# One core's GELU feed-forward: the last 64 rows of w1 loaded to both partition halves, tiles paired across halves, and w1's first piece cut by rows

## The chip, the cores and the metric

The kernel runs on one core of a Trainium2 chip. The metric is the device time of one execution in microseconds (us); of several runs the median counts. Below, PE is the matrix engine, PEld its weight loads, DVE the vector engine, ACT the scalar engine, POOL GpSimd, and SP the engine that issues most transfers. A transfer "lands" when its semaphore says that all of it has been written.

## The reference

```python
B, S, D, F = 1, 2048, 448, 1792          # all tensors bf16
h = jnp.einsum("bsd,df->bsf", x, w1) + b1
h = jax.nn.gelu(h, approximate=True)
out = jnp.einsum("bsf,fd->bsd", h, w2) + b2
```

D is 448, which is three blocks of 128 rows and 64 rows more. F is 14 blocks of 128.

## The kernel before, in words

**The work.** The 2048 tokens are taken in four chunks of 512 (SC). For a chunk, layer 1 makes 14 tiles of h (128 of F by 512 tokens), which go in seven pairs; a pair shares a unit of PSUM, and there are four units. ACT applies the GELU with the bias b1 and writes g. Layer 2 multiplies g by w2 for the chunk's four blocks of 128 tokens, DVE adds b2, and SP stores.

**Two halves.** Every matmul uses 64 rows: partitions 0 to 63 or 64 to 127. Two matmuls on different halves run side by side. So the two tiles of a pair always work on opposite halves: in pass "a" of `Layer1.step` tile lo works on one half, in pass "b" on the other. Rows 0 to 383 of w1 are three full blocks (k = 0, 1, 2), and both halves are needed by both tiles. The last 64 rows (k = 3) are a single half block, multiplied in pass "b" alone: one tile of the pair has them on the lower half of the partitions, the other on the upper half. The matching rows of x stand on both halves.

**The last 64 rows of w1 before.** `load_w1r` (line 135) brings them to partitions 64 to 127 alone, in two pieces (64 KB and 160 KB). The copies of line 399 on DVE then move the odd tiles of each piece to partitions 0 to 63 (events w1rU), since a pair is tiles 2j and 2j+1 and its odd tile works on the lower half in pass "b".

**Order.** Each engine has a list of operations that is written out by hand and carried out in order; an operation waits for the named events (`Program.emit`, line 45). A transfer has a semaphore of its own per event, and a wait is for the full count. The lists that matter here:

- SP, from line 153: x of chunk 0 (`xn`), then a barrier until ACT's table load is over, `load_w1r(0)`, `load_w1(2)` (tiles 4 to 7), `load_w1r(1)`, `load_w1(3)` (tiles 8 to 13), the two halves of w2, b2, and twelve transposing loads for x of chunks 1 to 3.
- ACT issues `load_w1(0)` (tiles 0, 1) and `load_w1(1)` (tiles 2, 3) at its start. POOL issues the load of b1.
- PE, from line 389: eight warming matmuls on ones (`warm`), the transposes of x (`turn_first`), pair 0's pass "a" on the first 256 tokens (HC), the rest of the transposes (`turn_rest`), pair 1's pass "a" on the same tokens, both passes on the next 256 tokens, then pass "b" of pairs 0 and 1, and from pair 2 on `L[j].a()` followed by `L[j - 1].b()`.
- DVE and ACT empty the transposes from PSUM into xT (`drain_blocks`, line 357, and line 384). DVE then does the first copy of line 399, the turning of b1 (`turn_b1`, line 179), and the second copy of line 399.

All matmuls of the two layers are recorded at line 217, the weight loads too; the transposes at line 344; the warming at line 192; the GELU at line 269.

Of the kernel before, what the change touches and what calls it, by code (L numbers as in the profile page):

```python
# [7 lines left out]
BF16 = mybir.dt.bfloat16  # L8
# [65 lines left out]
def bass_standalone__dense_activation_gelu__prompt_kernel(  # L74
# [8 lines left out]
    B, S, D = x.shape  # L83
    F = w1.shape[1]
    P = 128
    H = P // 2
    SC = 512
    HC = SC // 2
    assert B == 1 and S % SC == 0 and F == 14 * P and D == 3 * P + H
    x2, out2 = x[0], out[0]  # L90
    NSC, NST, STC, NFT = S // SC, S // P, SC // P, F // P
    NPAIR = NFT // 2
    KT = 3
    D3 = KT * P
# [3 lines left out]
    with ExitStack() as es:  # L98
        sb = lambda name, shape, dt: es.enter_context(nc.sbuf_tensor(name, shape, dt))
# [2 lines left out]
        ident = sb("ident", [P, P], BF16)  # L102
        xT = sb("xT", [P, KT + 1, S], BF16)
        w1_sb = sb("w1_sb", [P, KT, F], BF16)
        w1r = sb("w1r", [P, F], BF16)
        w2_sb = sb("w2_sb", [P, NFT, D], BF16)
        junk = sb("junk", [P, 1], BF16)
        b1n = sb("b1n", [32, P], BF16)
# [8 lines left out]
        pr = Program(nc, es)  # L117
# [2 lines left out]
        ones_m = one.broadcast_to([P, SC])  # L120


        W1CUTS = (0, 2, 4, 8, 14)

        def w1_of(ft):
            return max(i for i, c in enumerate(W1CUTS) if c <= ft)

        def load_w1(i, engine="sync"):
            c0, c1 = W1CUTS[i] * P, W1CUTS[i + 1] * P
            pr.dma(engine, lambda e: e.dma_start(  # L130
                w1_sb[:, :, c0:c1], w1[0:D3, c0:c1].rearrange("(k p) f -> p k f", p=P)), ("w1", i))

        RCUTS = (0, 4, 14)

        def load_w1r(i, engine="sync"):
            cs = slice(RCUTS[i] * P, RCUTS[i + 1] * P)
            pr.dma(engine, lambda e: e.dma_start(w1r[H:P, cs], w1[D3:D, cs]), ("w1r", i))

        def load_w2(a, b):
            pr.dma("sync", lambda e: e.dma_start(  # L140
                w2_sb[:, a:b, :], w2[a * P:b * P, :].rearrange("(f p) d -> p f d", p=P)), ("w2", a))
# [11 lines left out]
        pr.dma("sync", lambda e: e.dma_start(xn[:, :, :], x0v), "x")  # L153
        pr.barrier("sync", ["table"])
        load_w1r(0)
        load_w1(2)
        load_w1r(1)
        load_w1(3)
        load_w2(0, 7)
        load_w2(7, 14)  # L160
        pr.dma("sync", lambda e: e.dma_start(b2_bc[:, :], b2.partition_broadcast(P)), "b2")
        for c in range(1, NSC):
            for slot in range(KT + 1):
# [9 lines left out]
        pr.dma("gpsimd", lambda e: e.dma_start(b1n[0:NFT, :], b1.rearrange("(c p) -> c p", p=P)), "b1n",  # L173
               after=["b1z"])
        pr.op("scalar", lambda e: e.activation(junk[:, :], one, ACT.Gelu_apprx_tanh), event="table")  # L175
        load_w1(0, "scalar")
        load_w1(1, "scalar")

        def turn_b1():
            for q in range(4):  # L180
                pr.op("vector", lambda e, q=q: e.transpose(  # L181
                    b1t[32 * q:32 * q + 32, :], b1n[:, 32 * q:32 * q + 32]), after=["b1n"], event=("b1t", q))
            pr.op("vector", lambda e: e.tensor_copy(b1_f[:, :], b1t[:, 0:NFT]),
                  after=[("b1t", q) for q in range(4)], event="b1")
# [21 lines left out]
        def free(u):  # L206
            return [busy[(u, i)] for i in (0, 1, 2) if (u, i) in busy]

        def mm(u, lo, half, cols, lhsT, rhs, start, stop, after, event=None, skip=False):

            after = list(after)
            before = side.get((u, lo))
            if start:
                before = None
            if before is not None and before[0] != half:
                after.append(before[1])
            o = pr.op("tensor", lambda e: e.matmul(  # L217
                unit[u][:, lo, cols], lhsT=lhsT, rhs=rhs, start=start, stop=stop, skip_group_check=skip),
                after=after, event=event)
            side[(u, lo)] = (half, o)  # L220

        class Layer1:
# [6 lines left out]
            def step(self, part, k, t0=0, t1=SC):  # L229
                c, j, u = self.c, self.j, self.u  # L230
                s0 = c * SC
                for lo in (0, 1):
                    ft = 2 * j + lo
                    half = lo if part == "a" else 1 - lo
                    rows = slice(half * H, (half + 1) * H)
                    if k < KT:
                        lhsT = w1_sb[rows, k, ft * P:(ft + 1) * P]
                        after = [("w1", w1_of(ft))]
                    else:
                        lhsT = w1r[rows, ft * P:(ft + 1) * P]  # L240
                        after = [("w1r" if half else "w1rU", int(ft >= RCUTS[1]))]
                    if c == 0:
                        for h in range(t0 // HC, t1 // HC):
                            after += ([("xT0", h, k)] if k < KT else
                                      [("xR0", half, 0), ("xR0", half, 1)])
                    else:
                        after += [("xT", c), ("xTd", c)]
                    if self.fresh:
                        after += free(u)
                    fin = part == "b" and k == KT and t1 == SC  # L250
                    mm(u, lo, half, slice(t0, t1), lhsT, xT[rows, k, s0 + t0:s0 + t1], self.fresh, fin, after,
                       ("h", c, ft) if fin else None, self.skip)
                self.fresh = False
# [11 lines left out]
            def act(self):  # L265
                c, u = self.c, self.u
                for lo in (0, 1):
                    ft = 2 * self.j + lo
                    pr.op("scalar", lambda e, lo=lo, ft=ft: e.activation(  # L269
                        g[:, ft, c * SC:(c + 1) * SC], unit[u][:, lo, :], ACT.Gelu_apprx_tanh,  # L270
                        bias=b1_f[:, ft:ft + 1], scale=1.0), after=[("h", c, ft), "b1"], event=("g", c, ft))
                    busy[(u, lo)] = ("g", c, ft)
# [99 lines left out]
        def turn_rest():  # L372


            turn_block(1, 2, 2, 0, [("xT0", 0, 2)])
            for q in range(STC // 2):
                turn(lambda half, q=q: spot(2, 1)[:, half, q, :], lambda rows, q=q: xr[rows, q, :], ("xr", q), ["xr_in"])
            drain_blocks("vector", 1, (2,), 2, ("xr", 1))
            for src, engine in enumerate(("vector", "scalar")):
                i = spot(2, 1, HALVES[src])  # L380
                for dst in (src, 1 - src):
                    o = xT[HALVES[dst], KT, 0:SC].rearrange("p (q two b s) -> p b q two s", q=2, two=2, b=2)[:, :, :, src, :]
                    pr.op(engine, lambda e, o=o, i=i, engine=engine:
                          e.copy(o, i) if engine == "scalar" else e.tensor_copy(o, i),  # L384
                          after=[("xr", 1), ("xT0", 1, 2)], event=("xR0", dst, src))
            busy[(2, 1)] = ("xR0", 1, 0)
            busy[(2, 2)] = ("xR0", 0, 1)
# [2 lines left out]
        warm(1, HC)  # L390
        turn_first()
        L = [Layer1(0, j) for j in range(NPAIR)]
        L[0].a(0, HC)
        turn_rest()

        for i in (0, 1):
            odd = lambda rows, i=i: w1r[rows, RCUTS[i] * P:RCUTS[i + 1] * P].rearrange(
                "p (j two q) -> p j two q", two=2, q=P)[:, :, 1, :]
            pr.op("vector", lambda e, odd=odd: e.tensor_copy(odd(slice(0, H)), odd(slice(H, P))),
                  after=[("w1r", i)], event=("w1rU", i))  # L400
            if i == 0:
                turn_b1()
        L[1].a(0, HC)
        L[0].a(HC, SC)
        L[1].a(HC, SC)
        L[0].b()
# [7 lines left out]
        for c in range(NSC):  # L414
            if c:
                items = [Layer1(c, j) for j in range(NPAIR)]
                items[0].a()
                for j in range(1, NPAIR):
                    items[j].a()
                    items[j - 1].b()  # L420
                items[-1].b()
            else:

                pr.op("vector", lambda e: e.tensor_copy(b2_z[H:H + 1, :], b2_bc[H:H + 1, :]),  # L424
                      after=["b2", "b2z0"], event="b2z")
            if c + 1 < NSC:
                dup_x((c + 1) * SC, (c + 2) * SC, [("xT", c + 1)], ("xTd", c + 1))
            head, tail, every = range(0, 10), range(10, NFT), range(NFT)
            p = Layer2(c, (0, 1))
            if c + 1 < NSC:  # L430
                q = Layer2(c, (2, 3))
                for part in (head, tail):
                    p.part("a", part)
                    q.part("a", part)
                p.part("b", every)
                q.part("b", every)
            else:
                q, r = Layer2(c, (2,)), Layer2(c, (3,), True)
                p.part("a", every)
                q.part("a", every)  # L440
                p.part("b", every)
                r.bias()
                r.part("a", every)
                q.part("b", every)
                r.part("b", every)
# [30 lines left out]
```

## Time and profile before

| what | value |
|---|---|
| median of 11 runs | 93.89 us (93.82 to 94.46) |
| the profiled execution's own time | 93.82 us |
| its span, first to last instruction | 92.5 us |
| time around the span | 93.82 - 92.5 = 1.3 us |
| PE busy | 89.2 us, 945 matmuls |
| ACT busy / DVE busy | 38.4 us / 13.5 us |
| moved by DMA | 7.32 MB; HBM read 3.79 MB, written 1.84 MB |
| granted PE clock | 1.000 |

How to read it: the profile lists each engine's instructions with start and duration in us from the start of the span, and for idle time before an instruction it names what released it. A start in the table of line 217 is one matmul of a pair; its partner on the other half starts a few ns later, and durations of neighbours overlap, so progress on PE is read from the distance between starts, not from single durations. For transfers there are the issuing instruction (queue SPq, ACTq or POOLq), the time from issue to landing, and, behind the queue view, a record of every packet (one contiguous run moved by one DMA engine: start, duration, bytes) and of every landing (sixteen for a load, the last one releases the waiter).

### The profile page before, as it was taken

The page shows a single profiled execution, that of the slowest core. Times are in us where ns is not written, and L with a number is a line of the kernel's source. Part 1 is how long each engine was busy: PE and PEld are TensorE (multiplying, and loading weights), DVE is VectorE, ACT ScalarE, POOL GpSimd, SP SyncE. Part 2 cuts the span into 40 slices and gives each one's busy share as a digit, 9 for nine tenths or more (in the row PEclk, how much of TensorE's full clock was granted, in tenths as well). Part 3 has the DMA queues.
Part 4 walks back from the last instruction along what each step waited for, and adds up shares of the span by engine and source line. Part 5 has one row for each costly group of instructions (what it writes and reads, how often), then busy time and mean ns, then how long its engine had stood idle before and what let it go on. Part 6 is the DMA issues. An engine that isn't in the chain of part 4 may idle for free.

```text
span 92.5 us, 2086 instructions
## 1 busy us (share of the span) xinstructions
PE 89.2 (96%) x945; PEld 45.9 (50%) x945; DVE 13.5 (15%) x34; ACT 38.4 (41%) x64; POOL 1.7 (2%) x8
## 2 busy tenths in 40 slices
PE   6999999999999999999999999999999999999990
PEld 2374444555544444555544444555554444475890
DVE  0165000100541000000433000000333000000421
ACT  6074978600005788700003787900002888900001
POOL 6000000000000000000000000000000000000000
PEclk9999999999999999999999999999999999999999
DMA  1999995965757100000033000000022000000022
GB/s 31 348 276 325 372 316 72 175 108 96 54 105 204 50 7 0 0 0 0 0 102 104 0 4 0 7 0 0 0 99 99 7 0 0 0 0 7 26 73 99
DMA packets 12744, 7.32 MB, mean 79 GB/s; under 512 B 6976, under 2 KB 12544, under 8 KB 12736
## 3 DMA queue, kind: packets, MB, share of 16 engines
q1 hardware_dynamic: 11904, 6.80, 31.0%
q10 hardware_dynamic: 800, 0.39, 1.4%
q8 instruction: 7, 0.11, 0.5%
q0 software_dynamic: 32, 0.00, 0.0%
q14 instruction: 1, 0.01, 0.0%
HBM read 3.79 MB, written 1.84 MB: 61 GB/s over the span
## 4 chain that ended last, share of the span: by engine, by line
PE 96%; DVE 1%; issue 0%
PE u L217 92%; PE u L192 4%; PE u L344 0%; DVE out_sb L326 0%; DVE xT L357 0%
## 5 line engine op out<-in xcount | busy, mean ns | idle before, releaser
L269 ACT ACTIVATE g<-u,b_f 128x512 bf16<-128x512 f32 x56 | 34.9, 685 | 39.5 <-PE u L217 38.0
L217 PE MATMUL u<-w_sb,g 64*128 64x448 bf16 (+1 forms) x504 | 43.2, 328 | 0.0
L217 PE MATMUL u<-xT,w_sb 64*128 64x512 bf16 (+1 forms) x348 | 41.0, 369 | 0.2 <-DVE xT L357 0.2
L217 PEld LDWEIGHTS u<-w_sb,g 64*128 64x128 bf16 x504 | 24.5, 94 | 18.4
L217 PEld LDWEIGHTS u<-xT,w_sb 64*128 64x128 bf16 x348 | 16.8, 94 | 19.3 <-DMA w_sb<-in_w_dram 0.3
L312 DVE TENSOR_TENSOR out_sb<-u,b_bc 128x448 bf16<-128x448 f32 x14 | 8.1, 620 | 60.0 <-PE u L217 60.0
L217 PE MATMUL u<-xT,w1r 64*128 64x512 bf16 x56 | 10.6, 376 | 0.0
L217 PEld LDWEIGHTS u<-xT,w1r 64*128 64x128 bf16 x56 | 2.7, 94 | 3.3
L329 ACT CAST out_sb<-u 128x224 bf16<-128x224 f32 x1 | 0.3, 345 | 9.2 <-PE u L217 9.2
L192 PE MATMUL u<-const-bfloat16-1.0 128*128 128x512 bf16 (+1 forms) x8 | 3.4, 598 | 0.8 <-PEq L461 0.8
L192 PEld LDWEIGHTS u<-const-bfloat16-1.0 128*128 128x128 bf16 x8 | 1.0, 136 | 2.4 <-issue 2.4
L357 ACT COPY xT<-u 128x256 bf16<-128x256 bf16 x3 | 0.9, 381 | 2.4 <-PE u L344 2.4
L175 ACT ACT_TABLE_LOAD x1 | 1.3, 1283 | 0.7 <-PEq L461 0.7
L424 DVE COPY b_z<-b_bc 1x448 bf16<-1x448 bf16 x1 | 0.3, 268 | 7.1 <-DMA b_bc<-in_b_dram 7.1
L187 DVE COPY xT<-xT 64x512 bf16<-64x512 bf16 x3 | 0.9, 289 | 2.1 <-DMA xT<-in_x_dram 2.1
L344 PEld LDWEIGHTS u<-ident,xn 64*128 64x128 bf16 x24 | 0.7, 106 | 0.7 <-issue 0.7
L384 ACT COPY xT<-u 64x256 bf16<-64x256 bf16 x2 | 0.7, 368 | 0.5 <-DVE xT L357 0.5
L357 DVE COPY xT<-u 128x256 bf16<-128x256 bf16 x3 | 0.8, 289 | 0.8 <-PE u L344 0.8
L320 DVE TENSOR_TENSOR out_sb<-u,b_bc 128x448 bf16<-128x448 f32 x1 | 0.6, 625 | 1.7 <-PE u L217 1.7
L344 PE MATMUL u<-ident,xn 64*128 64x64 bf16 x24 | 0.8, 206 | 0.0
L181 DVE STREAM_TRANSPOSE b1t<-b1n 32x32 bf16<-32x32 bf16 x4 | 0.8, 201 | 0.1
L362 DVE COPY xr<-xn 128x256 bf16<-128x256 bf16 x1 | 0.2, 226 | 3.1 <-DMA xn<-in_x_dram 3.1
(18 smaller groups left out, 4.8 us busy)
## 6 DMA issues: line engine op xcount, KB each, us to landing
out_dram<-out_sb SPq DMA_DIRECT2D x16, 112.0 KB, 1.7
w_sb<-in_w_dram SPq DMA_DIRECT2D x2, 784.0 KB, 9.0
w_sb<-in_w_dram SPq DMA_DIRECT2D x1, 576.0 KB, 6.1
xn<-in_x_dram SPq DMA_DIRECT2D x1, 448.0 KB, 3.3
w_sb<-in_w_dram ACTq DMA_DIRECT2D x2, 192.0 KB, 4.1
w_sb<-in_w_dram SPq DMA_DIRECT2D x1, 384.0 KB, 5.2
xT<-in_x_dram SPq DMA_TRANSPOSE x12, 3.9
w1r<-in_w_dram SPq DMA_DIRECT2D x1, 160.0 KB, 5.1
```

The lines of the kernel that those rows point to most:

```text
L175: pr.op("scalar", lambda e: e.activation(junk[:, :], one, ACT.Gelu_apprx_tanh), event="table")
L181: pr.op("vector", lambda e, q=q: e.transpose(b1t[32 * q:32 * q + 32, :], b1n[:, 32 * q:32 * q + 32]), after=["b1n"], event=("b1t", q))
L187: pr.op("vector", lambda e: e.tensor_copy(xT[0:H, KT, s0:s1], xT[H:P, KT, s0:s1]), after=after, event=event)
L192: pr.op("tensor", lambda e: e.matmul(unit[0][:, 0, 0:cols], lhsT=ones_w, rhs=ones_m[:, 0:cols], start=True, stop=True))
L217: o = pr.op("tensor", lambda e: e.matmul(unit[u][:, lo, cols], lhsT=lhsT, rhs=rhs, start=start, stop=stop, skip_group_check=skip), after=a ...
L269: pr.op("scalar", lambda e, lo=lo, ft=ft: e.activation(g[:, ft, c * SC:(c + 1) * SC], unit[u][:, lo, :], ACT.Gelu_apprx_tanh, bias=b1_f[:, ...
L312: pr.op("vector", lambda e, lo=lo, j=j: e.tensor_tensor(out=out_sb[:, j, :], in0=unit[u][:, lo, 0:D], in1=b2_bc[:, :], op=ALU.add), after= ...
L320: pr.op("vector", lambda e: e.tensor_tensor(out=out_sb[:, j, :].rearrange("p (two h) -> p two h", two=2), in0=unit[u][:, :, 0:DH], in1=b2_ ...
L329: pr.op("scalar", lambda e: e.copy(out_sb[:, j, DH:D], unit[u][:, 1, 0:DH]), after=[y[1]], event=("o", j, 1))
L344: pr.op("tensor", lambda e, half=half, rows=rows: e.transpose(o(half), i(rows), ident[rows, rows]), after=["ident"] + after, event=event i ...
L357: pr.op(engine, lambda e, i=i: (e.copy if engine == "scalar" else e.tensor_copy)(o[:, i], f[:, i]), after=[wait or ("xt", h, ks[-1])], eve ...
L384: e.copy(o, i) if engine == "scalar" else e.tensor_copy(o, i),
```

## The change

1. **w1's last 64 rows** go to all 128 partitions by the load itself: the piece's columns are cut in two, the first half to partitions 0 to 63, the second half to partitions 64 to 127. `w1r` is now indexed by pair. The copies of line 399 are gone. There are three pieces instead of two (pairs 0-1, 2-3 and 4-6), with runs of 512, 512 and 768 bytes.
2. **Pairs** follow from that: PAIRS takes one tile of each half of the piece, and the halves of passes "a" and "b" are swapped. Layer 2 goes through its tiles in the order in which the pairs make them (ORDER).
3. **w1's first piece** is tiles 0 to 3 instead of 0 and 1, and it is loaded in two transfers by rows: block k = 0 (128 KB), then blocks 1 and 2 (256 KB). PE's start goes by blocks: k = 0 for pairs 0 and 1, k = 1 for both, `turn_rest`, k = 2 for both.
4. DVE's list has the turning of b1 straight after the drains.

The transfer that the new `load_w1r` builds for its first piece walks w1 as 2 column halves x 64 rows x 256 elements and writes 128 partitions x 256 elements. All other plain loads, before and after, walk both sides with 128 partitions outermost, and the old `load_w1r` with 64 (b1's, on POOL, with 14).

```diff
-        w1r = sb("w1r", [P, F], BF16)
+        w1r = sb("w1r", [P, NPAIR, P], BF16)
...
-        W1CUTS = (0, 2, 4, 8, 14)
+        W1CUTS = (0, 4, 8, 14)
...
-        def load_w1(i, engine="sync"):
+        def load_w1(i, engine="sync", k0=0, k1=KT):
             c0, c1 = W1CUTS[i] * P, W1CUTS[i + 1] * P
             pr.dma(engine, lambda e: e.dma_start(
-                w1_sb[:, :, c0:c1], w1[0:D3, c0:c1].rearrange("(k p) f -> p k f", p=P)), ("w1", i))
-
-        RCUTS = (0, 4, 14)
+                w1_sb[:, k0:k1, c0:c1], w1[k0 * P:k1 * P, c0:c1].rearrange("(k p) f -> p k f", p=P)), ("w1", i, k0))
+        PAIRS = ((0, 2), (1, 3), (4, 6), (5, 7), (8, 11), (9, 12), (10, 13))
+        ORDER = [ft for pair in PAIRS for ft in pair]
+        RCUTS = (0, 2, 4, 7)
+        def w1r_of(j):
+            return max(i for i, c in enumerate(RCUTS) if c <= j)
         def load_w1r(i, engine="sync"):
-            cs = slice(RCUTS[i] * P, RCUTS[i + 1] * P)
-            pr.dma(engine, lambda e: e.dma_start(w1r[H:P, cs], w1[D3:D, cs]), ("w1r", i))
+            j0, j1 = RCUTS[i], RCUTS[i + 1]
+            rows = w1[D3:D, 2 * j0 * P:2 * j1 * P]
+            pr.dma(engine, lambda e: e.dma_start(
+                w1r[:, j0:j1, :], rows.rearrange("r (two c) -> two r c", two=2)), ("w1r", i))
...
         load_w1r(0)
+        load_w1(1)
+        load_w1r(1)
         load_w1(2)
-        load_w1r(1)
-        load_w1(3)
+        load_w1r(2)
...
-        load_w1(0, "scalar")
-        load_w1(1, "scalar")
+        load_w1(0, "scalar", 0, 1)
+        load_w1(0, "scalar", 1)
...
-                    ft = 2 * j + lo
-                    half = lo if part == "a" else 1 - lo
+                    ft = PAIRS[j][lo]
+                    half = 1 - lo if part == "a" else lo
...
-                        after = [("w1", w1_of(ft))]
+                        after = [("w1", w1_of(ft), int(ft < W1CUTS[1] and k > 0))]
                     else:
-                        lhsT = w1r[rows, ft * P:(ft + 1) * P]
-                        after = [("w1r" if half else "w1rU", int(ft >= RCUTS[1]))]
+                        lhsT = w1r[rows, j, :]
+                        after = [("w1r", w1r_of(j))]
...
-        L[0].a(0, HC)
-        turn_rest()
-
-        for i in (0, 1):
-            odd = lambda rows, i=i: w1r[rows, RCUTS[i] * P:RCUTS[i + 1] * P].rearrange(
-                "p (j two q) -> p j two q", two=2, q=P)[:, :, 1, :]
-            pr.op("vector", lambda e, odd=odd: e.tensor_copy(odd(slice(0, H)), odd(slice(H, P))),
-                  after=[("w1r", i)], event=("w1rU", i))
-            if i == 0:
-                turn_b1()
-        L[1].a(0, HC)
+        for k in range(KT):
+            if k == 2:
+                turn_rest()
+            for j in (0, 1):
+                L[j].step("a", k, 0, HC)
+        turn_b1()
...
-            head, tail, every = range(0, 10), range(10, NFT), range(NFT)
+            head, tail, every = ORDER[:10], ORDER[10:], ORDER
```

More of the change, by code (lines that the diff above doesn't have):

```diff
@@ L267, in act @@
                 for lo in (0, 1):
-                    ft = 2 * self.j + lo
+                    ft = PAIRS[self.j][lo]
                     pr.op("scalar", lambda e, lo=lo, ft=ft: e.activation(
```

## The prediction, put on record before the changed kernel ran

> **What bounds the kernel now.** I read the shares first, then the chain, then PE's starts at the head, then the transfers. The page:
>
> ```profile
> PE 89.2 (96%) x945; PEld 45.9 (50%) x945; DVE 13.5 (15%) x34; ACT 38.4 (41%) x64; POOL 1.7 (2%) x8
> PE   6999999999999999999999999999999999999990
> DMA  1999995965757100000033000000022000000022
> ```
>
> PE is full from the second slice to the last but one; the transfers are full only in the first ten slices (23 us). The chain, in order of time:
>
> ```profile
> 4.51 0.30 DVE xT L357
> 4.81 0.14 issue
> 4.95 0.50 PE u L217 x6
> 5.45 0.12 PE u L344 x8
> 5.57 0.01 issue
> 5.58 84.75 PE u L217 x903
> 90.33 0.38 DVE out_sb L326
> ```
>
> From 5.58 us on PE never stops. A pair of 256-column matmuls takes 0.109 us from start to start, a pair of 512 columns 0.215, and the change leaves count and columns of all matmuls as they are. So it can gain only before 5.58, and lose wherever PE comes to stand later. One wait lies in the head, seen in the weight loads between 4.9 and 5.7 us:
>
> ```profile
> 5.30 0.14 PEld L344 LDWEIGHTS u<-ident,xr 64*128 64x128 bf16 x4
> 5.58 0.11 PEld L217 LDWEIGHTS u<-xT,w_sb 64*128 64x128 bf16 x4
> ```
>
> The transposes' last matmul starts at 5.38; the next, pair 1's first, waits until w1's tiles 2 and 3 land at 5.54 and starts at 5.58. Without the wait it would start at 5.40: 0.18 us to be had. Now the transfers (issue to landing), with issues and PE's start at the place that matters, from the timeline:
>
> ```profile
> w_sb<-in_w_dram SPq DMA_DIRECT2D x1, 576.0 KB, 6.1
> w_sb<-in_w_dram SPq DMA_DIRECT2D x1, 384.0 KB, 5.2
> w1r<-in_w_dram SPq DMA_DIRECT2D x1, 160.0 KB, 5.1
> w1r<-in_w_dram SPq DMA_DIRECT2D x1, 64.0 KB, 3.6
> ```
>
> ```profile
> 2.85 0.58 SPq L130 DMA_DIRECT2D w_sb<-in_w_dram  x1
> 4.01 0.59 SPq L130 DMA_DIRECT2D w_sb<-in_w_dram  x1
> 10.46 1.46 PE L217 MATMUL u<-xT,w_sb 64*128 64x512 bf16 x12
> ```
>
> Tiles 4 to 7 land at 2.85 + 5.2 = 8.07 us and are used at 8.30; tiles 8 to 13 land at 4.01 + 6.1 = 10.08 and are used at 10.46. The margins are 0.2 and 0.4 us: that is what a slower queue has to eat first.
>
> **The change, part by part.** (a) *DVE.* The two copies of line 399 (0.22 and 0.35 us) go. They lie beside a running PE: worth 0. ACT's first GELU waits 1.4 us for b1 while PE runs on; b1 a little earlier moves nothing either. The new pair order and swapped halves change no count: 0. The longer SP list (one issue more, 0.5 us by its neighbours) delays the x loads of chunk 1, which land at 18.4 and are used at 26.3: hidden by 8 us. POOL's list is unchanged.
>
> (b) *w1's first piece by rows.* By the packet records, sixteen engines move 512 B in 27 ns each, 1024 B in 46, 1536 B in 65, 2560 B in 102. Tiles 0 to 3 were 768 packets of 512 B, 48 per engine, 48 x 27 = 1.30 us; they become 384 of 1024 B, 24 x 46 = 1.10. So I estimate the second piece's landing at 5.54 - 0.19 = 5.35 (not earlier: 5.54). The first piece is 128 KB instead of 192 and lands before the 4.69 of its forerunner, in time for 4.95. New order on PE: k = 0 from 4.95, two pairs, done at 5.17. k = 1 needs the second piece, 5.35 + 0.05 (5.54 to 5.58 before) = 5.39 = R. Behind that wait stand, in PE's order, `turn_rest` and all else. From R: k = 1 0.22, eight transposes 0.125, k = 2 0.22, next 256 tokens, k = 0 and 1, 0.22, which is R + 0.78. The next matmul needs `turn_rest`'s block drained. Before, the last transpose started at 5.38, DVE's drain at 5.63, took 0.29, and PE could go on some 0.08 later: 0.62 after that transpose, which is now at R + 0.32. So R + 0.94: a new stall of 0.17. Before, ten matmuls (0.54) and the wait lay between; now eight (0.43). Then four pairs, 0.43: the first 512-column matmul at R + 1.38 = 6.77, against 6.58. This part loses 0.19 us; with the landing at 5.54 it loses 0.38; with R at 5.17 or less it gains 0.04. It breaks even with a landing at 5.16.
>
> The Trainium skill ("DMA: Bandwidth & Descriptors", Specifications) puts full rate at 512 B and up; by that the longer runs would save nothing and this part would lose 0.38 us, while the packet records above (19 against 22 bytes per ns) favour 0.19.
>
> (c) *The last 64 rows to both halves.* In before every load has sixteen landings, and the plain loads that SP and ACT issue have 128 or 64 as outermost count on both sides, which sixteen divides. The new load's source has 2 outermost. No row shows how such a load is spread. Bounds: sixteen engines, 128 / 16 = 8 packets of 512 B, 0.22 us, as now; or shared out by that outermost step, two engines with 64 packets each, 64 x 27 = 1.73 us. I take two engines: a division along the outermost step is what fits all the rows, and two does not divide by sixteen.
>
> The Trainium skill says it outright (same page, "Why a DMA increments its semaphore by 16 and not by 1"): the number of engines is the largest up to 16 that divides both sides' slowest dimension other than 1. That gives 2 here, and no run of before shows it; with sixteen, the sum would be part (b) alone.
>
> Each load waits its turn in its engine's queue: the packets of SP's first weight load start at 4.46, when ACT's are nearly through, though issued at 2.26. So what SP issues after these pieces waits on the two engines. Packets per engine up to the end of tiles 8 to 13: before 4 x 46 (w1r, 64 KB), 24 x 46, 4 x 102 (w1r, 160 KB), 24 x 65 ns = 3.26 us. After, on the two engines: 64 x 27, 24 x 46, 64 x 27, 24 x 65 = 6.12. That is 2.86 more, less the 0.19 of part (b): 2.67 us later. Tiles 8 to 13 landed at 8.6 to 9.1 on eleven of the sixteen engines (median 8.9) and at 9.8 to 10.1 on five. On the two engines that becomes 8.9 + 2.67 = 11.57 (from 11.25 to 12.75). PE wants them at 10.46 + 0.19; it starts 0.06 after the landing, 11.63. Queued behind this wait on PE: pair 4's pass "a" and everything after, pair 3's ready pass "b" too. The end moves by 11.63 - 10.46 = **1.17 us**, and part (b)'s 0.19 is inside that, not on top.
>
> What else is late, all by the same packets: the first last-rows piece lands at 6.65 to 7.24 (before 5.30 to 5.89, plus 1.54, less 0.19), wanted at R + 2.02 = 7.41; tiles 4 to 7 at 7.7 to 8.35, wanted at 8.49; the second last-rows piece at 9.7 to 10.3, wanted at 10.43; the third (64 packets of 768 B, some 36 ns between the rows of 512 and 896 B, 2.3 us) at 13.9, wanted at 14.4; w2's second half, then 5.0 later than before, at 18.0 (before 13.05 by the median engine), wanted at 17.18 + 1.17 = 18.35. All fit by 0.1 to 0.5 us; each can add some tenths if it is late. SP's issues may be held while the two engines' queues are long (b2's took 2.88 us before); the two engines have work meanwhile, so it costs nothing here. x of chunk 1 then lands by 23.4, still before 27.
>
> **Sum.** The profiled execution: 92.5 span + 1.3 around = 93.82. 93.82 + 1.17 = 94.99; I say 95.0. The profiled execution lies 0.07 under the median of the runs, within their spread.
>
> **Rivals.** *Two engines, and one of them slow* (the 9.8 to 10.1 rows): landing at 12.75, PE at 12.81, +2.35, 96.2. For it: five of sixteen were slow in that load. Against: long packets (up to 1.0 us instead of 65 ns) came at single moments. *Sixteen engines, first piece late*: part (b) alone, 94.0 (to 94.2). For it: the destination has 128 partitions, and all loads so far went sixteen ways. *Not slower*: sixteen engines, and w1's second piece lands by 5.16, so that k = 1 follows k = 0 without a wait: 93.8. It decides at 5.16; a landing 0.4 us earlier than now is twice what the packets give. *It doesn't do what it says*: had the wait of 0.18 gone and the drain not stalled, it would be 93.6, still within 0.3%. For more gain I see no place in the profile.
>
> **How the numbers follow.** About 0.3% (0.28 us) is what a measurement of this kernel can tell from no change. Two engines, as summed: 0.65, 95.0 (own range 94.67 to 95.3). Two engines and slow: 0.12. Sixteen, late piece: 0.14, of which 0.03 lose over 0.28. Not slower: 0.04. Faster in a way that I don't see: 0.05. So slower 0.65 + 0.12 + 0.03 = 0.80, within 0.11 + 0.04 = 0.15, faster 0.05. The range takes in sixteen engines as a bound of the unknown: 93.95 to 96.2.
>
> **What would show it.** In the profile after: PE idle at about 10.7, before pair 4's first matmul, released by the transfer of tiles 8 to 13; the landings of `w1r` in two, not sixteen, and the issue-to-landing time of the pieces up by 1 us and more; PE waiting at 5.17 to 5.4 for w1's second piece, then 0.17 for DVE's drain. I am wrong if `w1r` lands in sixteen shares, or if PE shows no gap between 8 and 19 us; then the head alone decides.

## The result, and the profile after

The changed kernel takes 95.47 us (median of 13 runs, 94.56 to 96.44), the kernel before 93.99 (50 runs, 93.71 to 94.46). The ratio is 1.0125, 95% interval 1.0103 to 1.0147: 1.2 us slower. Here and below, a ratio leaves out runs more than 1.5% above the fastest of the same kernel (four of the changed one's), so it is not quite the quotient of the medians, which here lie 1.5 us apart. The changed kernel's runs spread over 1.9 us, those of before over 0.75. The profiled execution took 95.21 us, span 93.9.

The page of the kernel after (busy time by engine, then tenths in 40 slices):

```profile
PE 89.2 (95%) x945; PEld 45.5 (48%) x945; DVE 12.9 (14%) x32; ACT 38.4 (41%) x64; POOL 1.7 (2%) x8
...
PE   6889699999999999999999999999999999999990
...
DMA  2958799785655620000033000000022000000022
```

PE is as busy as before, 89.2 us: the work is the same and the time is all waiting. The new dents are in the second to fifth slices, before 12 us. The end of the chain of waits (start, length, what):

```profile
3.46 0.57 SPq L145
4.03 0.04 issue
4.07 7.72 DMA w_sb<-in_w_dram
11.79 0.05 issue
11.84 79.88 PE u L227 x849
91.72 0.38 DVE out_sb L336
```

Before, the chain went back through PE to the first warming matmul. Now it leaves PE at 11.84 us, in the transfer of tiles 8 to 13, which SP issued at 4.07 and which landed at 11.79. The head no longer has a part in it. The issue of that transfer alone took 2.53 us of SP's time (0.59 before):

```profile
4.07 2.53 SPq L130 DMA_DIRECT2D w_sb<-in_w_dram  x1
```

The weight loads and matmuls about the two larger waits, from the timeline (idle time before, and who ended it, in brackets):

```profile
7.58 0.10 PEld L227 LDWEIGHTS u<-xT,w1r 64*128 64x128 bf16 x2 [0.59 <-DMA w1r<-in_w_dram]
```

```profile
10.61 0.38 PE L227 MATMUL u<-xT,w1r 64*128 64x512 bf16 x2
...
11.83 0.98 PEld L227 LDWEIGHTS u<-xT,w_sb 64*128 64x128 bf16 x12 [1.34 <-DMA w_sb<-in_w_dram]
11.84 1.47 PE L227 MATMUL u<-xT,w_sb 64*128 64x512 bf16 x12 [0.85 <-DMA w_sb<-in_w_dram]
```

PE would have gone on at 10.83 (10.61 and one pair of 0.215) and starts at 11.84. The transfers, in KB and us from issue to landing:

```profile
w_sb<-in_w_dram SPq DMA_DIRECT2D x1, 576.0 KB, 7.7
...
w_sb<-in_w_dram SPq DMA_DIRECT2D x1, 384.0 KB, 5.5
...
w1r<-in_w_dram SPq DMA_DIRECT2D x2, 64.0 KB
...
w1r<-in_w_dram SPq DMA_DIRECT2D x1, 96.0 KB
```

The `w1r` lines have lost their last column, because it is taken from loads with sixteen landings. The landing records of the first piece are three: one at 3.32, 1.06 us after the issue began and before any of its packets, then 7.46 and 7.53. Two engines moved it. The load of tiles 8 to 13 landed on fourteen engines at 9.78 to 10.15 and on two at 11.72 and 11.79.

### The profile page after: what moved, and what is told of

It is laid out like the page before. It is cut to its first block, busy times and chain, and to the rows that moved or that the text cites. A ratio compares the mean times of both kernels' runs of the same rounds, so it can differ in the third digit from the quotient of the medians.

```text
span 93.9 us, 2084 instructions
## 1 busy us (share of the span) xinstructions
PE 89.2 (95%) x945; PEld 45.5 (48%) x945; DVE 12.9 (14%) x32; ACT 38.4 (41%) x64; POOL 1.7 (2%) x8
## 4 chain that ended last, share of the span: by engine, by line
PE 85%; DMA 8%; SPq 2%; ACT 1%; issue 1%; ACTq 0%; DVE 0%
PE u L227 85%; DMA w_sb<-in_w_dram 8%; SPq L145 1%; ACT L185 0%; ACTq L130 0%; SPq L130 0%; DVE out_sb L336 0%; ACT junk L185 0%
```

## The experiments

**Sixteen engines instead of two.** Each piece is brought by two plain loads of 64 rows:

```diff
-            pr.dma(engine, lambda e: e.dma_start(
-                w1r[:, j0:j1, :], rows.rearrange("r (two c) -> two r c", two=2)), ("w1r", i))
+            for half in (0, 1):
+                cs = slice(half * (j1 - j0) * P, (half + 1) * (j1 - j0) * P)
+                pr.dma(engine, lambda e, half=half, cs=cs: e.dma_start(
+                    w1r[half * H:(half + 1) * H, j0:j1, :], rows[:, cs]), ("w1r", i))
```

> The changed kernel, but each piece of the last 64 rows is brought by two plain loads of 64 rows, one to each half of the partitions; bytes, run lengths and everything else stay. Theory (the load whose source has 2 outermost is moved by two engines, and tiles 8 to 13 queue behind it there): the landings come in sixteen shares, tiles 8 to 13 land at 10.0 to 10.3 us instead of 11.79, the gap of PE at 10.6 goes, and the time falls by 1.0 to 1.1 us to 94.0 to 94.2, what is left over the kernel before being the head. Rival (the bytes, the short runs or the additional transfers cost it, however they are spread): the time stays at 95.0 or above.

Measured: 94.38 us (expected 94.0 to 94.2), ratio 1.0029 (1.0009 to 1.0050), so about 0.9 of the 1.2 us go with nothing changed but the form of the loads. All these loads now have sixteen landings. Bytes and runs are the same: that rival falls. But 0.3 us stay, and tiles 8 to 13 landed at 10.99, not at 10.0 to 10.3. SP issued them later:

```profile
3.49 0.59 SPq L130 DMA_DIRECT2D w_sb<-in_w_dram  x1
4.12 1.14 SPq L147 DMA_DIRECT2D w1r<-in_w_dram  x2
5.30 0.59 SPq L130 DMA_DIRECT2D w_sb<-in_w_dram  x1
```

The two more issues put that of tiles 8 to 13 at 5.30 instead of 4.01. Yet that did not set the time of this execution: weight loads waited 0.16 us for the landing, PE did not, and the chain goes back through PE to the landing of x:

```profile
0.75 3.49 DMA xn<-in_x_dram
...
5.14 1.04 PE u L229 x8
...
6.38 84.67 PE u L229 x901
```

What sets the time can be read from the profiles together. In the seven in which PE waits for no transfer behind its first 512-column matmul (before, this one, and five of the versions below), the profiled time is that matmul's start plus 87.24 to 87.28 us: 6.58 and 93.82 before, 7.30 and 94.55 here. In the six in which PE waits for tiles 8 to 13, it is the start of their first matmul plus 83.35 to 83.37: 11.84 and 95.21 in the changed kernel. In these thirteen the later of the two sums is the time. So what is left here, in this execution, is the head, which ran at half the pace for a while (last section).

**The same move within the queue.** The changed kernel, with the second piece behind tiles 8 to 13:

```diff
-        load_w1r(1)
         load_w1(2)
+        load_w1r(1)
         load_w1r(2)
```

> The changed kernel with one move in SP's list: the second piece of the last 64 rows is issued behind tiles 8 to 13 instead of ahead of them. Theory (the two engines work off their queue in the order of issue): tiles 8 to 13 land 1.7 us earlier, near 10.1, and the second piece lands where they did, near 11.8; PE's gap moves to the matmuls on the last rows of pair 2, which stand 0.2 us ahead of pair 4's first in its order, so the time is 0.2 to 0.5 us above the changed kernel's, 95.3 to 95.6. Rival (the large load is slow by itself, in HBM): tiles 8 to 13 stay near 11.8 and the time does not move.

Measured: tiles 8 to 13 landed at 9.77 and the last-rows piece at 11.27. The gap moved as the queue's order says, and the large load is not slow by itself:

```profile
11.31 0.10 PEld L227 LDWEIGHTS u<-xT,w1r 64*128 64x128 bf16 x2 [0.80 <-DMA w1r<-in_w_dram]
```

The time was a miss: 94.66 us, ratio 1.0072 (1.0048 to 1.0096), below the changed kernel and not above it. The late landing came at 11.27 here and at 11.79 there, half a microsecond that I had taken as fixed. Why the same two queues finish at different times in two executions is not settled. One difference is in the packet records: in the changed kernel's profile no packet of the first last-rows piece starts between 5.53 and 6.11 us, on either engine; here and in the next two versions they have no such pause, and that piece landed at 7.33, 6.58 and 6.74 instead of 7.53.

**The cost doubled, on two engines and on sixteen.** The changed kernel with 64 KB loaded once more ahead of tiles 8 to 13, to a tile that nothing reads:

```diff
+        pr.dma("sync", lambda e: e.dma_start(
+            spare[:, :, :], w1[D3:D, 4 * P:8 * P].rearrange("r (two c) -> two r c", two=2)), "spare")
         load_w1(2)
```

> The changed kernel with the suspected cost doubled: the second piece of the last 64 rows is loaded once more, to a tile that nothing reads, by a load of the same form, ahead of tiles 8 to 13. Theory (64 more packets of 512 B on the two engines, 27 ns each, 1.73 us): tiles 8 to 13 land near 13.5, PE's gap grows by 1.7, the time is 1.6 to 1.8 us above the changed kernel's, 96.7 to 96.9. Rival (the bytes cost it, on whatever engines): 64 KB more are 0.2 us.

The control brings the same bytes by two loads of 64 rows:

```diff
+        for half in (0, 1):
+            pr.dma("sync", lambda e, half=half: e.dma_start(
+                spare[half * H:(half + 1) * H, :, :], w1[D3:D, (4 + 2 * half) * P:(6 + 2 * half) * P]), "spare")
         load_w1(2)
```

> As e7_two_again, but the additional 64 KB come as two loads of 64 rows. Theory (they spread over sixteen engines, 8 packets each, 0.22 us): 0.1 to 0.4 us above the changed kernel, 95.2 to 95.5. Rival (it is the bytes or the number of loads): as e7_two_again.

From the end of the chain, first with the load on two engines, then with it on sixteen:

```profile
5.54 7.61 DMA w_sb<-in_w_dram
13.15 0.05 issue
13.20 79.88 PE u L230 x849
```

```profile
6.41 5.24 DMA w_sb<-in_w_dram
11.64 0.05 issue
11.69 79.88 PE u L231 x849
```

On two engines, tiles 8 to 13 land at 13.15, 1.36 later than in the changed kernel; on sixteen, at 11.64, no later. In the doubled one the second piece landed on the two engines at 9.04 and 9.80 and the spare one at 10.68 and 11.66: 1.64 and 1.86 us for 64 packets each of 27 ns (1.73). In time: 96.16 us, ratio 1.0212 (1.0162 to 1.0261), 0.8 us above the changed kernel and not the 1.6 to 1.8 expected. In the profiles a part of the added cost is made up by the first piece, which landed at 6.58 here and at 7.53 in the changed kernel; whether that holds for the other runs isn't known. The control takes 95.27 us, within the expected 95.2 to 95.5, ratio 1.0168 (1.0102 to 1.0233), whose interval overlaps those of both others. The times of these four runs each tell little; the landings tell the two apart.

The length behind the landing, 79.88 us for 849 matmuls, is the same in all three. So the end is the landing of tiles 8 to 13 plus a constant, and a late head hides in that wait.

**The first piece by rows, alone.** The kernel before with part 3 of the change only:

```diff
-        L[0].a(0, HC)
-        turn_rest()
+        for k in range(KT):
+            if k == 2:
+                turn_rest()
+            for j in (0, 1):
+                L[j].step("a", k, 0, HC)
```

(with the cuts, the loads and the wait of the change).

> The kernel before with only the first piece of w1 changed: tiles 0 to 3, loaded by rows (k = 0, then k = 1 and 2), and PE's start by blocks; the last 64 rows, the pairs and DVE's copies as before. Theory (all of the loss comes from the last 64 rows): within 0.15 us of the sum for this part as the changed kernel's profile has it, 0.1 us slower than before (x lands some 0.15 later, the wait of 0.18 goes, a stall of some 0.17 for DVE's drain comes): 94.0 to 94.2, and no gap behind 8 us. Rival (the head costs a good part of the 1.2 us): 94.4 or more.

Measured: 94.39 us, above the 94.0 to 94.2 expected and just under the rival's 94.4; ratio 1.0018 (0.9997 to 1.0040), 0.17 us and not to be told from nothing. The medians of that round lie 0.35 apart. Its profile has no gap behind 8 us. So the head is not the bulk of the 1.2 us, but it may be up to a third of it, and it can be all of the 0.3 us that the sixteen-engine loads leave: this version, with SP's issues as before, is not measurably faster than that one.

**The rest of the transposes earlier**, on top of the sixteen-engine loads:

```diff
-            if k == 2:
+            if k == 1:
                 turn_rest()
```

> As e1_sixteen, but the rest of the transposes stands before k = 1 instead of before k = 2. Theory (the stall after k = 2 is DVE's drain, which starts with the last transpose): the drain starts 0.2 us earlier, the stall of 0.17 goes, 0.15 to 0.2 us faster than e1_sixteen, 93.8 to 94.0. Rival (the stall comes from the load of w1's second piece): as e1_sixteen.

Measured: 94.31 us (expected 93.8 to 94.0), ratio 1.0020 (1.0001 to 1.0038), not to be told from the sixteen-engine loads. The stall after the drain is not in the profile, but it isn't in theirs either, whose head ran slowly; so this run doesn't test what the move is worth. In the profiled execution tiles 8 to 13 (issued at 5.30, landed at 11.26) held PE, so a shorter head could not have shown there:

```profile
5.30 5.96 DMA w_sb<-in_w_dram
11.26 0.05 issue
11.30 79.88 PE u L229 x849
```

**x and w1 on one queue**, on top of that: both loads of w1's first piece are issued by SP straight behind x.

```diff
-        load_w1(0, "scalar", 0, 1)
-        load_w1(0, "scalar", 1)
...
+        load_w1(0, "sync", 0, 1)
+        load_w1(0, "sync", 1)
         pr.barrier("sync", ["table"])
```

> As e4_rest_early, but w1's first piece is issued by SP straight behind x, on x's own queue, instead of by ACT. Theory (in the changed kernel x landed at 4.22 instead of 4.05 because packets of w1 got in between its own): x lands at 4.0 to 4.1, the first matmul on x starts at 4.95, w1's second piece lands by 5.25; 0.1 to 0.15 us faster than e4_rest_early, 93.7 to 93.9. Rival (x's landing varies by itself): no difference.

Measured: 94.41 us (expected 93.7 to 93.9), ratio 1.0046 (1.0024 to 1.0068): slower than before, and not faster than the version it was built on. x did land at 3.90 instead of 4.35, but w1's second piece landed at 5.50, not by 5.25, and PE waited for it. In this execution tiles 8 to 13, landing at 11.38, set the end again, so the profile doesn't tell what the earlier x is worth.

**As many issues on SP as before.** The earlier-transposes version, with the lower halves of the first two pieces issued by ACT:

```diff
-        load_w1r(0)
+        load_w1r(0, "sync", (1,))
...
-        load_w1r(1)
+        load_w1r(1, "sync", (1,))
...
+        load_w1r(0, "scalar", (0,))
+        load_w1r(1, "scalar", (0,))
```

> As e4_rest_early, but the loads of 64 rows to the lower half, for the first two pieces, are issued by ACT behind w1's first piece, so that SP has as many issues ahead of tiles 8 to 13 as in the kernel before. Theory (what sixteen-engine loads still lose is SP's time: two more issues of 0.59 us put the issue of tiles 8 to 13 at 5.30 instead of 4.01 and their landing at 11.0 to 11.4 instead of 10.1): the issue comes at 4.0, the landing at 10.1 to 10.4, the gap of PE at 10.9 goes, 0.1 to 0.3 us faster than e4_rest_early, 93.9 to 94.1. Rival (the loss is in the head, x landing late): no difference to e4_rest_early, 94.3.

Measured: 94.06 us, as expected, ratio 0.9993 (0.9971 to 1.0016): no loss that can be told. From the earlier-transposes version (1.0001 to 1.0038) it isn't clear of noise either, and its head was short in the profile too (first 512-column matmul at 6.44), so what SP's issues cost by themselves stays open. Tiles 8 to 13 were issued at 4.03 and landed at 9.94; the weight loads run through pair 4's first without a wait:

```profile
9.89 0.11 PEld L231 LDWEIGHTS u<-xT,w1r 64*128 64x128 bf16 x2
10.11 0.97 PEld L231 LDWEIGHTS u<-xT,w_sb 64*128 64x128 bf16 x10
```

This kernel has every part of the change, with the loads in another form and `turn_rest` one block earlier.

**DVE's copies alone taken away** (pairs, cuts and order of before; two loads of 64 rows per piece, one of them on ACT):

```diff
+            rows = w1[D3:D, RCUTS[i] * P:RCUTS[i + 1] * P].rearrange("r (j two q) -> r j two q", two=2, q=P)
+            pr.dma(engine, lambda e: e.dma_start(
+                w1r[half * H:(half + 1) * H, RCUTS[i] // 2:RCUTS[i + 1] // 2, :], rows[:, :, 1 - half, :]), ("w1r", i, half))
```

> The kernel before with only DVE's copies taken away: the last 64 rows go to both halves by loads of 64 rows, the lower half's issued by ACT, in the pairs 2j and 2j+1 and with runs of 256 B; w1's first piece, its cuts and PE's order as before. Theory (the copies lie beside a running PE): no difference, 93.9 to 94.1. Rival (the copies hold up b1 or the last rows): 0.2 us or more faster.

Measured: 93.92 us, ratio 0.9994 (0.9967 to 1.0020). The copies, which ran beside PE, were worth nothing that can be told.

**The wait of before filled.** Three versions that the profiles point to. First, one move on PE:

```diff
-        L[1].a(0, HC)
-        L[0].a(HC, SC)
+        L[0].step("a", 0, HC, SC)
+        L[1].a(0, HC)
+        L[0].step("a", 1, HC, SC)
+        L[0].step("a", 2, HC, SC)
```

> The kernel before with one move on PE: pair 0's first block on the second 256 tokens stands ahead of pair 1's pass a, which waits for w1's tiles 2 and 3. It changes no transfer. Theory (the wait of 0.18 us is real and one pair of 0.109 us fits into it): 0.1 us faster than before, 93.8 to 93.95. Rival (the clock's rise and x's landing decide the head): no difference that can be told.

Measured: 93.91 us, ratio 0.9985 (0.9962 to 1.0008), not to be told from before. Its profile shows the next limit, in the weight loads:

```profile
9.71 0.10 PEld L217 LDWEIGHTS u<-xT,w1r 64*128 64x128 bf16 x2
10.66 0.33 PEld L217 LDWEIGHTS u<-xT,w_sb 64*128 64x128 bf16 x6 [0.85 <-DMA w_sb<-in_w_dram]
```

Second, tiles 8 to 13 in two loads as well:

```diff
-        W1CUTS = (0, 2, 4, 8, 14)
+        W1CUTS = (0, 2, 4, 8, 10, 14)
...
+        load_w1(4)
```

> As e12_fill_the_wait, and tiles 8 to 13 come as tiles 8, 9 and tiles 10 to 13 in two loads on SP. Theory (what a better head gains is given back at pair 4, since the end is set by the later of the head and the landing of tiles 8 to 13, 10.61 us in the profile of e12_fill_the_wait with a gap of 0.63): tiles 8, 9 land by 9.3, no gap at pair 4, 0.1 to 0.3 us faster than before, 93.7 to 93.9. Rival (the head alone sets the end in most executions): as e12_fill_the_wait.

Third, with the copies taken away too:

> As e13_two_limits, and the last 64 rows loaded to both halves as in e10_copies_alone, without DVE's copies. Theory (the copies are worth nothing): as e13_two_limits, within 0.1 us. Rival (the additional loads take the transfers' time at the head): 0.1 us or more slower than e13_two_limits.

Measured: 93.78 us, ratio 0.9981 (0.9954 to 1.0007), and 93.75 us, ratio 0.9972 (0.9945 to 0.9998). Neither profile has a gap at pair 4. The last is the only kernel here whose interval lies below 1, and just so; among twelve versions that is weak evidence of a gain.

## Why the prediction was right, step by step

- **Two engines: right, and most of the loss.** Two landings of `w1r` in place of sixteen; one load made two takes 0.9 of 1.2 us away. The version with SP's issues as few as before has no loss that can be told; how the last 0.3 us divide between the head and SP's issues is not shown. The landing records agree with the Trainium skill's rule ("DMA: Bandwidth & Descriptors", "Why a DMA increments its semaphore by 16 and not by 1"), also in that the issuer writes the missing counts at once: the one landing at 3.32 us.
- **Size: right within 0.2 us in the profile, 0.5 short in the median.** Tiles 8 to 13 at 11.79 (said 11.57, 11.25 to 12.75); PE's start at 11.84 (said 11.63). In the profiles the end moved by 95.21 - 93.82 = 1.39 (said 1.17); by the ratio, 1.2. But the median of the runs, 95.47, lies above the 95.0 and above the 94.67 to 95.3 given to two engines; it is the wider range, kept for the unknown, that takes it in. The prediction has no term for the spread of the runs, and what makes it so wide is not shown.
- **That part (b) lies inside that wait: right.** 79.88 us behind the landing, whatever the head did. With the first 512-column matmul at 6.67, the head alone would have given 6.67 + 87.25 = 93.92.
- **Part (b), size 0.19: its terms were partly wrong.** w1's second piece landed at 5.09, not 5.35: no wait for it at all. The stall for DVE's drain came, 0.15 us (said 0.17). What I missed is x: it landed at 4.22 instead of 4.05. ACT's packets begin at 2.77 us now (before 3.12) and x's last one starts at 3.68 (3.53). In all, the first 512-column matmul started 0.1 later than before (6.67 against 6.58). The experiment on part 3 alone gives 0.17 (-0.03 to 0.38). The other profiles bear that out: in the eight in which ACT loads w1's first piece by rows, x landed at 4.11 to 4.35; in the five in which ACT loads it as before, at 3.66 to 4.05; with both on one queue, at 3.90. That packets of w1 get between those of x is the likely reason.
- **"All fit by 0.1 to 0.5 us": wrong for the first last-rows piece.** It landed at 7.53 (said 6.65 to 7.24), after the pause of 0.58 us in its packets, and PE waited 0.26 at 7.3. It cost nothing, since the larger wait follows.
- **SP held while two queues are long: right, and right that it costs nothing here.** The issue of tiles 8 to 13 took 2.53 us (4.07 to 6.60) instead of 0.59, and the fourteen other engines landed that load at 9.8 to 10.2, where eleven engines landed it at 8.6 to 9.1 before. PE could use it from 10.83 on. In the doubled version that issue ended at 8.27 and the fourteen landed at 11.6 to 11.8, behind the 10.8 at which PE was ready: there the late issue alone would have made PE wait.
- **Copies worth 0: right as far as it can be told** (0.9994, 0.9967 to 1.0020).

## What to carry to other kernels

Before a load is put in another form, ask over how many DMA engines it is spread: a source whose outermost step has count 2 was moved by two of sixteen, and everything behind it in the queue waited there. Two plain loads of 64 rows cost one more issue of 0.6 us on their engine, so put them where that engine has time. And price an edit by what sets the end at that place: with PE full behind it, the end was the landing of one load plus a constant, and what was saved on DVE or lost in the head did not show. Where no load held PE, the head set the end, microsecond for microsecond.

## What I had not expected of the hardware

The PE clock rises at quite different times. In the profile of before a pair of 256-column matmuls took 0.109 us from 5.58 on. With the sixteen-engine loads, pairs took 0.213 from 5.33 to 6.58; the timeline there:

```profile
5.14 1.04 PE L229 MATMUL u<-xT,w_sb 64*128 64x256 bf16 x8
5.94 0.34 PE L356 MATMUL u<-ident,xn 64*128 64x64 bf16 x4
```

Eight matmuls of 256 columns take 0.80 us from their start to the next group's, where the changed kernel's eight, from 5.07 to 5.50, take 0.43. From the first of them to the first 512-column matmul it is 2.16 us (5.14 to 7.30), in the changed kernel 1.60 (5.07 to 6.67). Where the profiles record the rise, it came at 3.62, 3.89, 4.44, 5.06, 5.15 and 6.05 us, in six kernels whose PE all started warming at 0.78. So a late rise costs, by estimate from these two heads, up to half a microsecond; the 93.7 to 94.5 us of the kernel before may come from it, which was not tried. The Trainium skill ("TensorE: Matmul & The Clock Gate", Part 1: The HAM clock gate) has the gate watch a window of some 3.4 us that runs free of the kernel's start; the spread of the rise here, 2.4 us, would fit that, but it is wider than the 500 ns to either side that the same section gives.
